# The last 272 token columns of a closing two-matmul stage: second product with the weights stationary, in place of two token tiles and a 16-column strip

## The chip, the cores and the metric

The kernel runs on one NeuronCore of a Trainium2 chip. The metric is the device time of one execution in microseconds; the time before is the median of three runs. One further execution was recorded by the profiler, and all rows below come from it. PE is TensorE (matmuls), PEld its weight loads, DVE is VectorE, ACT is ScalarE, POOL is GpSimd, SP issues DMAs.

## The reference

Three stages follow one another: attention with rotary embedding, a top-1 mixture of eight experts, and a two-matmul stage. Only the last is touched by the change:

```python
def _moe2_ref(x, w_in, w_out, alpha):        # x 1152x512, w_in 512x2048, w_out 2048x512, float64 weights
    h = x @ w_in
    g = np.maximum(h, 0.0) + alpha * np.minimum(h, 0.0)
    return (g @ w_out).astype(np.float32)
```

A token that its expert had no room for has a row of zeros, so only the tokens that were kept need this stage. In the path that runs here they fill at most 784 columns.

## The kernel before

All of the closing stage is in `ffn` (made by `make_ffn`). The tokens stand as columns: `yh` holds the 512 features of up to 784 tokens, split into a high and a low part. Each product runs in three passes (high by high, high by low, low by high), the tuple `PASS`.

**The first product** is `up(f)`, for f from 0 to 15: 128 of the 2048 hidden features at a time, the weights stationary, the tokens moving in three blocks of 272, 256 and 256 columns. One block is 12 matmuls into one of four PSUM banks. ACT reads the bank twice (L1133, L1134: the positive and the negative part into temporary tiles of `room`), DVE joins the two with alpha (L1136), ACT rounds the result to the high part of g (L1141), and POOL forms the low part (L1142). g of one f lies in one of five slots (`g01`, `split_room`).

**The second product** is `down(mg)`, for mg from 0 to 3: four f at a time, with g stationary. A token tile is 128 columns of g; 12 matmuls with 512 columns of w_out moving make its 128 x 512 partial output in one PSUM bank, and DVE scales it and adds it to an accumulator (L1198, L1200). There are six tiles, 0 to 5, and they go round three banks, `acc[0]` to `acc[2]`: tile 3 can start when DVE has read tile 0, tile 4 when it has read tile 1.

**The strip.** 784 is six tiles and 16 columns. The 16 columns (`STRIP`) are kept unsplit in float32: POOL copies them out of the third block (L1146), and `down_strip`, behind tile 0 of each `down`, multiplies them with the unsplit w_out in four column groups of the array (L1157), into the fourth bank, `acc[3]`. Only then may the next w_out block be loaded over the unsplit one (`load2`). In the last `down` ACT copies the bank out (L1166) and a matmul with the 0/1 matrix `fold` adds the four column groups (L1171, behind tile 3). `fold` is made by a DVE reduction in the first microseconds of the program (L993).

**The weights** arrive as float64. A piece, `split2`, makes 128 x 512 of them usable: three DVE instructions turn the bits into float32 (L1020, L1021, L1022), ACT rounds them (L1025), POOL forms the low part (L1026). There are 24 pieces in this path of the stage. `pace()` is called behind each block of `up` and each tile of `down`, and every second call puts one piece into the queues (`piece`); four of the pieces fall within each of the first three `down`s and the last `up` ahead of it, none into the last `down`.

**The order.** Every engine runs its queue in the order in which the code writes it. The stage is up(0) to up(4), down(0), up(5) to up(8), down(1), up(9) to up(12), down(2), up(13) to up(15), down(3). In down(3) each finished tile is scattered to the rows of `out` by an indirect DMA that POOL issues (L598). Below, down(0) to down(3) are called the first to the fourth pass.

## Time and profile before

| what | value |
|---|---|
| median of 3 runs | 464.43 us (464.12 to 465.53) |
| the profiled execution's own time | 468.51 us |
| its span, first to last instruction | 466.7 us |
| mean granted TensorE clock | 0.982 |
| PE busy | 421.9 us, 90% |
| DVE busy | 305.5 us, 65% |
| ACT busy | 216.1 us, 46% |
| POOL busy | 238.7 us, 51% |
| closing stage | from 302.07 us to the end |

A share of busy time is an average over stages with different limits. The closing stage has three kinds of stretches: those of the first product, the first three passes of the second product with weight pieces on DVE beside them, and the fourth pass without. What ends a wait is read in each by itself. A row of the order of time gives the start in us, the duration in us, engine, line, operation, the tiles written and read, the shape, the count, and in brackets the idle time before it with the instruction that ended it.

### The profile page before, as it was taken

The page shows a single profiled execution, that of the slowest core. Times are in us where ns is not written, and L with a number is a line of the kernel's source. Part 1 is how long each engine was busy: PE and PEld are TensorE (multiplying, and loading weights), DVE is VectorE, ACT ScalarE, POOL GpSimd, SP SyncE. Part 2 cuts the span into 40 slices and gives each one's busy share as a digit, 9 for nine tenths or more (in the row PEclk, how much of TensorE's full clock was granted, in tenths as well). Part 3 has the DMA queues.
Part 4 walks back from the last instruction along what each step waited for, and adds up shares of the span by engine and source line. Part 5 has one row for each costly group of instructions (what it writes and reads, how often), then busy time and mean ns, then how long its engine had stood idle before and what let it go on. Part 6 is the DMA issues. An engine that isn't in the chain of part 4 may idle for free. (4 is left out here: it accounts for less than half of the span.)

```text
span 466.7 us, 8223 instructions
## 1 busy us (share of the span) xinstructions
PE 421.9 (90%) x2993; PEld 332.2 (71%) x2993; DVE 305.5 (65%) x563; ACT 216.1 (46%) x540; POOL 238.7 (51%) x280
## 2 busy tenths in 40 slices
PE   6789999999989999995878798998999899889993
PEld 3576666666666666695867798697689589758962
DVE  8996566574777464579489911139888797886321
ACT  2476767666665667342253331164424514432600
POOL 6578482864775334148645310047736745662532
PEclk9999999999999999999899898999999999999998
DMA  7422999604031624467466667940314045000012
GB/s 215 129 60 48 175 332 295 185 1 121 0 119 35 195 88 160 158 228 250 104 208 216 235 222 264 374 170 1 122 60 180 5 178 183 0 1 0 2 69 73
DMA packets 37329, 63.71 MB, mean 137 GB/s; under 512 B 9886, under 2 KB 16158, under 8 KB 37280
## 3 DMA queue, kind: packets, MB, share of 16 engines
q1 hardware_dynamic: 35424, 58.83, 39.7%
q0 software_dynamic: 1568, 3.95, 2.3%
q8 instruction: 25, 0.41, 0.4%
q10 hardware_dynamic: 288, 0.33, 0.2%
q14 instruction: 24, 0.20, 0.1%
HBM read 47.35 MB, written 11.65 MB: 126 GB/s over the span
## 5 line engine op out<-in xcount | busy, mean ns | idle before, releaser
L308 DVE TENSOR_REDUCE nm<-S 128x1 f32<-128x576 f32 x72 | 54.2, 755 | 45.0 <-PE S L299 27.7
L309 ACT ACTIVATE P<-S,nm 128x576 f32<-128x576 f32 x72 | 53.5, 742 | 52.6 <-DVE nm L308 51.0
L1124 PE MATMUL u_a<-yh,whl 128*128 128x256 f32 (+1 forms) x576 | 71.3, 284 | 6.1 <-ACT room L1134 5.7
L1124 PEld LDWEIGHTS u_a<-yh,whl 128*128 128x128 f32 x576 | 70.1, 188 | 7.4 <-ACT room L1134 6.4
L1136 DVE SCALAR_TENSOR_TENSOR room<-room,nal 128x256 f32<-128x256 f32 (+1 forms) x48 | 30.5, 637 | 30.9 <-ACT room L1134 30.8
L330 PEld LDWEIGHTS pt<-ident,P 128*128 128x128 f32 x256 | 27.0, 141 | 29.3 <-ACT P L309 6.8
L1026 POOL TENSOR_TENSOR whl<-wraw,whl 128x512 fp32r<-128x512 f32 x22 | 28.9, 1312 | 35.8 <-ACT whl L1025 32.7
L363 PE MATMUL av<-PT,v 128*64 128x288 f32 x256 | 44.7, 431 | 0.4 <-DVE PT L319 0.3
L1188 PE MATMUL acc<-whl,split_room 128*128 128x512 f32 x162 | 42.3, 396 | 2.2 <-DVE xs L1200 1.2
L330 PE MATMUL pt<-ident,P 128*128 128x128 f32 x256 | 41.5, 286 | 3.1 <-ACT P L309 2.9
L1025 ACT CAST whl<-wraw 128x512 fp32r<-128x512 f32 x22 | 14.5, 657 | 54.2 <-DVE wraw L1022 54.2
L1188 PEld LDWEIGHTS acc<-whl,split_room 128*128 128x128 f32 x162 | 29.7, 188 | 13.1 <-DVE xs L1200 2.9
L1142 POOL TENSOR_TENSOR g<-room,g 128x272 fp32r<-128x272 f32 (+2 forms) x21 | 17.7, 853 | 41.7 <-ACT g L1141 39.2
L299 PE MATMUL S<-T,T 128*128 128x288 f32 x112 | 36.1, 338 | 1.1 <-DVE T L178 1.1
L1188 PE MATMUL acc<-whl,g 128*128 128x512 f32 x126 | 32.9, 391 | 0.5 <-POOL whl L1026 0.5
L299 PE MATMUL S<-X,T 128*128 128x288 f32 x112 | 31.2, 293 | 0.0
L154 POOL TENSOR_TENSOR hl<-R,hl 128x512 fp32r<-128x512 f32 x12 | 15.4, 1287 | 30.6 <-ACT hl L153 30.5
L1142 POOL TENSOR_TENSOR split_room<-room,split_room 128x272 fp32r<-128x272 f32 (+2 forms) x27 | 24.6, 919 | 12.3 <-ACT split_room L1141 9.5
L1188 PEld LDWEIGHTS acc<-whl,g 128*128 128x128 f32 x126 | 23.5, 188 | 6.6 <-POOL whl L1026 0.9
L319 DVE COPY PT<-pt 128x512 f32<-128x512 f32 (+1 forms) x32 | 19.9, 623 | 12.2 <-PE pt L330 7.9
L319 ACT COPY PT<-pt 128x512 f32<-128x512 f32 (+1 forms) x48 | 26.0, 544 | 3.6 <-PE pt L330 3.4
L927 POOL TENSOR_TENSOR whl<-wraw,whl 128x512 fp32r<-128x512 f32 x12 | 15.9, 1329 | 22.3 <-ACT whl L924 22.3
(290 smaller groups left out, 925.4 us busy)
## 6 DMA issues: line engine op xcount, KB each, us to landing
wraw<-moe_w SPq DMA_DIRECT2D x16, 1024.0 KB, 6.3
wraw<-moe_w_out SPq DMA_DIRECT2D x3, 2048.0 KB, 8.1
x_disp<-zero SPq DMA_DIRECT2D x9, 576.0 KB, 8.0
wraw<-moe_w_in SPq DMA_DIRECT2D x2, 2048.0 KB, 10.1
X<-T SPq DMA_DIRECT2D x14, 288.0 KB, 4.1
room<-moe_w SPq DMA_DIRECT2D x3, 1024.0 KB, 6.5
out<-zero SPq DMA_DIRECT2D x4, 576.0 KB, 7.9
v<-v SPq DMA_DIRECT2D x8, 256.0 KB, 5.2
```

Of the source, the lines that this page charges most:

```text
L299: nc.tensor.matmul(ps[:, half, 0:288], lhsT=lhsT, rhs=rhs, start=(n == 0), stop=(n == len(terms) - 1),)
L308: nc.vector.tensor_reduce(nm, ps[:, :, 0:288], op=ALU.max, axis=AX.XY, negate=True)
L309: nc.scalar.activation(Pt.rearrange("p (a n) -> p a n", a=2), ps[:, :, 0:288], AF.Exp, bias=nm, scale=1.0, accum_out=st["ssum"][:, t, hh : ...
L319: (nc.vector.tensor_copy if SCH["e"][k] else nc.scalar.copy)(o, i)
L330: nc.tensor.transpose(ps[:, kb, :], Pt[:, at : at + 128], ident)
L363: nc.tensor.matmul(ps[64 * hh : 64 * hh + 64, 0:288], lhsT=lhs, rhs=(PT[:, hh, kb] if kb < 4 else PR)[:, half * 288 : half * 288 + 288], s ...
L927: eng.tensor_tensor(ht[:, 1, c], rt[:, c], ht[:, 0, c].bitcast(F32), op=ALU.subtract)
L1026: nc.gpsimd.tensor_tensor(ht[:, 1, c], hw.bitcast(F32), ht[:, 0, c].bitcast(F32), op=ALU.subtract)
L1124: nc.tensor.matmul(ps, lhsT=wt[:, a, c, (f % 4) * 128 : (f % 4) * 128 + 128], rhs=yh_[0][:, b, c, c0 + lo : c0 + hi], start=(c == 0 and i ...
L1136: nc.vector.scalar_tensor_tensor(A, Bn, nal[:, f : f + 1], A, op0=ALU.mult, op1=ALU.add)
L1142: nc.gpsimd.tensor_tensor(g_cols(g, 1, lo, mid), A[:, 0 : mid - lo], hi_.bitcast(F32), op=ALU.subtract)
L1188: nc.tensor.matmul(ps[:m], lhsT=g_cols(g, b, t * P, t * P + m), rhs=wt[:, a, c, :], start=(c == 0 and i == 0), stop=(c == 3 and i == 2),)
```

## The change

The three blocks of the first product become 256, 256 and 272 columns. The 16 columns are no longer held apart: the last block of 272 columns (`TURN`) is split into high and low parts like the others, and the g slots are 784 columns wide instead of 768. Tiles 0 to 3 stay as they were. In place of tiles 4, 5 and the strip, `down_turned` runs behind tile 1 of each pass: for each d of four 128-column groups of w_out, 12 matmuls with w_out stationary and the 272 columns of g moving make a 128 x 272 block of the transposed output, and DVE adds it to the accumulator `accT`. All groups go round four banks instead of three. In the fourth pass, ahead of tile 3, `finish_turned` transposes `accT` back on PE, four 128 x 128 transposes for each of tiles 4, 5 and 6 (the last with 16 rows), DVE scales each, and POOL scatters it. `pace()` is called as often as before in each pass. The loads of w_out no longer wait for the strip, the reduction for `fold` is gone, and the memory that was zeroed for the strip by DVE is replaced by a part of `accT` zeroed by POOL.

```diff
+TURN = 256 + STRIP
...
-        nc.vector.tensor_reduce(
-            fold, ident.rearrange("p (g m) -> p m g", m=32)[:, 0:STRIP], op=ALU.add, axis=AX.X
-        )
...
-                            if c == 3 and not (strip and g % 2):
+                            if c == 3:
                                 later.append(lambda: load2(seq.index(g) + 2))
...
-                                if mid < hi:
-                                    nc.gpsimd.tensor_copy(gs[:, f // 4 % 2, f % 4, 0:STRIP], A[:, mid - lo : hi - lo])
...
+                    def down_turned(mg):
+
+                        wt = w2_hl(2 * mg + 1)
+                        for d in range(4):
+                            ps = po(f"t_{tag}_{mg}_{d}")[:, 0:TURN]
+                            for c in range(4):
+                                g = gt[(4 * mg + c) % NG]
+                                for i, (a, b) in enumerate(PASS):
+                                    nc.tensor.matmul(
+                                        ps,
+                                        lhsT=wt[:, a, c, d * 128 : d * 128 + 128],
+                                        rhs=g_cols(g, b, c_t, n_all),
+                                        start=(c == 0 and i == 0),
+                                        stop=(c == 3 and i == 2),
+                                    )
+                            flush()
+                            o = accT[:, d, 0:TURN]
+                            if mg == 0:
+                                nc.vector.tensor_copy(o, ps)
+                            else:
+                                nc.vector.tensor_tensor(o, ps, o, op=ALU.add)
+                            if d % 2:
+                                pace()
+
+                    def finish_turned(t, m):
+
+                        at = t * P - c_t
+                        ps = po(f"y_{tag}_{t}")
+                        for d in range(4):
+                            nc.tensor.transpose(ps[:, d * 128 : d * 128 + 128], accT[:, d, at : at + 128], ident)
+                        y = A_y[t][:m]
+                        nc.vector.tensor_scalar(y, ps[:m], wgt[:m, t, 0:1], None, op0=ALU.mult)
+                        finish(t, m, y)
...
                         for t, m in tiles:
-                            if strip and t == 1:
-                                down_strip(mg)
+                            if turned and t == 2:
+                                down_turned(mg)
+                            if mg == 3 and t == 3:
+                                for last in turned:
+                                    finish_turned(*last)
...
-                                if strip and t == 3:
-                                    finish_strip()
...
-                    ffn(0, (272, 256, 256), "a", False, (0, 1))
+                    ffn(0, (256, 256, TURN), "a", False, (0, 1))
...
-                u, d = itertools.cycle(("h", "xt")), itertools.cycle(range(3))
+                u, d = itertools.cycle(("h", "xt")), itertools.cycle(range(4))
```

The third pass on PE, before: acc_2502, acc_2503 and acc_2504 are the three banks, acc_2505 the strip's, whl the split weights, g and split_room the slots of g.

```order
L1188 MATMUL acc_2502<-whl_2101,split_room 128x512 x6
L1188 MATMUL acc_2502<-whl_2101,g_2104 128x512 x6
L1157 MATMUL acc_2505<-wraw_2100,room 32x512 x4
L1188 MATMUL acc_2503<-whl_2101,split_room 128x512 x6
L1188 MATMUL acc_2503<-whl_2101,g_2104 128x512 x6
L1188 MATMUL acc_2504<-whl_2101,split_room 128x512 x6
L1188 MATMUL acc_2504<-whl_2101,g_2104 128x512 x6
L1188 MATMUL acc_2502<-whl_2101,split_room 128x512 x6
```

The same pass on PE now, from tile 1 to the first half of tile 2; the four banks are acc_2500 to acc_2503, and tile 0, not shown, is in acc_2500.

```order
L1196 MATMUL acc_2501<-whl_2099,split_room 128x512 x6
L1196 MATMUL acc_2501<-whl_2099,g_2102 128x512 x6
L1154 MATMUL acc_2502<-split_room,whl_2099 128x272 x6
L1154 MATMUL acc_2502<-g_2102,whl_2099 128x272 x6
L1154 MATMUL acc_2503<-split_room,whl_2099 128x272 x6
L1154 MATMUL acc_2503<-g_2102,whl_2099 128x272 x6
L1154 MATMUL acc_2500<-split_room,whl_2099 128x272 x6
L1154 MATMUL acc_2500<-g_2102,whl_2099 128x272 x6
L1154 MATMUL acc_2501<-split_room,whl_2099 128x272 x6
L1154 MATMUL acc_2501<-g_2102,whl_2099 128x272 x6
L1196 MATMUL acc_2502<-whl_2099,split_room 128x512 x6
```

Behind tile 0 the strip is gone; tile 1 and two short groups now come ahead of the group that takes tile 0's bank again.

DVE in the third pass, before, from the reading of tile 0 (acc_2502) to that of tile 5; the rows on wraw are weight pieces.

```order
L1200 SCALAR_TENSOR_TENSOR xs<-acc_2502,room,xs 128x512
L1020 TENSOR_SCALAR cv<-wraw_2483 128x512
L1021 SCALAR_TENSOR_TENSOR wraw_2483<-wraw_2483,cv 128x512
L1022 SCALAR_TENSOR_TENSOR wraw_2483<-wraw_2483 128x512
L1200 SCALAR_TENSOR_TENSOR xs<-acc_2503,room,xs 128x512
L1200 SCALAR_TENSOR_TENSOR xs<-acc_2504,room,xs 128x512
L1020 TENSOR_SCALAR cv<-wraw_2483 128x512
L1021 SCALAR_TENSOR_TENSOR wraw_2483<-wraw_2483,cv 128x512
L1022 SCALAR_TENSOR_TENSOR wraw_2483<-wraw_2483 128x512
L1200 SCALAR_TENSOR_TENSOR room<-acc_2502,room 128x512
L1200 SCALAR_TENSOR_TENSOR room<-acc_2503,room 128x512
L1200 SCALAR_TENSOR_TENSOR room<-acc_2504,room 128x512
```

DVE in the same pass now, from the reading of tile 1 (acc_2501) to that of tile 3.

```order
L1208 SCALAR_TENSOR_TENSOR xs<-acc_2501,room,xs 128x512
L1166 TENSOR_TENSOR room<-acc_2502,room 128x272
L1166 TENSOR_TENSOR room<-acc_2503,room 128x272
L1017 TENSOR_SCALAR cv<-wraw_2481 128x512
L1018 SCALAR_TENSOR_TENSOR wraw_2481<-wraw_2481,cv 128x512
L1019 SCALAR_TENSOR_TENSOR wraw_2481<-wraw_2481 128x512
L1166 TENSOR_TENSOR room<-acc_2500,room 128x272
L1166 TENSOR_TENSOR room<-acc_2501,room 128x272
L1208 SCALAR_TENSOR_TENSOR xs<-acc_2502,room,xs 128x512
L1208 SCALAR_TENSOR_TENSOR room<-acc_2503,room 128x512
```

The place of the pieces among the readings stays: one behind the reading of tile 0, one behind the reading of bank 3.

The end of the fourth pass on PE now, from the third short group: tile 2, the transposes of tiles 4, 5 and 6, and tile 3.

```order
L1154 MATMUL acc_2500<-split_room,whl_2100 128x272 x9
L1154 MATMUL acc_2500<-g_2102,whl_2100 128x272 x3
L1154 MATMUL acc_2501<-split_room,whl_2100 128x272 x9
L1154 MATMUL acc_2501<-g_2102,whl_2100 128x272 x3
L1196 MATMUL acc_2502<-whl_2100,split_room 128x512 x9
L1196 MATMUL acc_2502<-whl_2100,g_2102 128x512 x3
L1175 MATMUL acc_2503<-ident,room 128x128 x4
L1175 MATMUL acc_2500<-ident,room 128x128 x4
L1175 MATMUL acc_2501<-ident,room 128x128 x4
L1196 MATMUL acc_2502<-whl_2100,split_room 128x512 x9
L1196 MATMUL acc_2502<-whl_2100,g_2102 128x512 x3
```

Five of the seven scatters, of tiles 2, 4, 5, 6 and 3 in this order, now stand behind the last two tiles; before, each of the seven stood behind a tile of its own or the `fold` matmul.

## Rows read from the trace of the kernel before

**Rows 1.** The page, busy time of each engine over the span (us, share, instructions).

```profile
PE 421.9 (90%) x2993; PEld 332.2 (71%) x2993; DVE 305.5 (65%) x563; ACT 216.1 (46%) x540; POOL 238.7 (51%) x280
```

**Rows 2.** Busy us by stretch (PE, PEld, DVE, ACT, POOL), granted clock, DMA: third, fourth pass.

```profile
405.00:427.00 22.00, 19.50 (x83) 13.57 (x82) 18.42 (x24) 7.21 (x18) 12.20 (x12) 1.00 0.00 1
...
440.00:460.00 20.00, 19.24 (x85) 13.71 (x83) 5.85 (x9) 1.94 (x5) 8.12 (x10) 1.00 0.18 67
```

**Rows 3.** Order of time on PE, second pass: strip, tile 1, next first product.

```profile
369.55 1.10 PE L1157 MATMUL acc<-wraw,room 128*32 128x512 f32 x6
...
372.03 0.98 PE L1188 MATMUL acc<-whl,split_room 128*128 128x512 f32 x3
...
385.80 14.65 PE L1124 MATMUL u_a<-yh,whl 128*128 128x272 f32 x120
```

**Rows 4.** Order of time on PE, third pass: strip, tiles 1 and 4, next first product.

```profile
408.68 1.10 PE L1157 MATMUL acc<-wraw,room 128*32 128x512 f32 x6
...
411.59 1.66 PE L1188 MATMUL acc<-whl,split_room 128*128 128x512 f32 x6
...
421.56 1.65 PE L1188 MATMUL acc<-whl,split_room 128*128 128x512 f32 x6 [0.80 <-DVE xs L1200]
...
427.13 13.16 PE L1124 MATMUL u_a<-yh,whl 128*128 128x272 f32 x108
```

**Rows 5.** Order of time on DVE: readings of tiles 0, 1 and 2, a piece's start.

```profile
374.40 0.74 DVE L1200 SCALAR_TENSOR_TENSOR xs<-acc,room,xs 128x512 f32<-128x512 f32 x1
...
378.22 1.41 DVE L1200 SCALAR_TENSOR_TENSOR xs<-acc,room,xs 128x512 f32<-128x512 f32 x2
...
416.96 0.74 DVE L1200 SCALAR_TENSOR_TENSOR xs<-acc,room,xs 128x512 f32<-128x512 f32 x1
417.62 1.38 DVE L1020 TENSOR_SCALAR cv<-wraw 128x512 uint32<-128x512 uint32 x1
...
420.76 1.40 DVE L1200 SCALAR_TENSOR_TENSOR xs<-acc,room,xs 128x512 f32<-128x512 f32 x2
```

**Rows 6.** Order of time on PE, fourth pass: strip, tiles 2 and 3, fold.

```profile
442.95 1.26 PE L1157 MATMUL acc<-wraw,room 128*32 128x512 f32 x8
...
447.00 2.20 PE L1188 MATMUL acc<-whl,split_room 128*128 128x512 f32 x9
...
449.72 2.20 PE L1188 MATMUL acc<-whl,split_room 128*128 128x512 f32 x9
...
452.53 1.03 PE L1171 MATMUL acc<-wraw,fold 128*16 128x512 f32 x2
```

**Rows 7.** Order of time on PE in the attention: four float32 transposes.

```profile
151.34 0.66 PE L330 MATMUL pt<-ident,P 128*128 128x128 f32 x4
```

**Rows 8.** Order of time: last reading on DVE, its scatter, and scatters in a row.

```profile
229.45 0.97 POOL L598 DMA_INDIRECT meta_d<-g_meta,m_mi  x1 [0.30 <-issue]
...
459.27 0.75 DVE L1200 SCALAR_TENSOR_TENSOR room<-acc,room 128x512 f32<-128x512 f32 x1 [1.97 <-PE acc L1188]
...
460.30 0.97 POOL L598 DMA_INDIRECT out<-room  x1 [1.73 <-POOLq L1604]
```

**Rows 9.** Order of time on DVE at the program's start: the fold reduction.

```profile
3.82 0.26 DVE L993 TENSOR_REDUCE fold<-ident 128x16 f32<-128x64 f32 x1
```

**Rows 10.** Costliest groups on the page (count, busy us, mean ns, idle before): POOL copies, whole stage.

```profile
L1146 POOL COPY room<-room 128x16 f32<-128x16 f32 x16 | 7.4, 462 | 0.0
```

**Rows 11.** PE idle stretches in order of time, and the stretch after each, as Rows 2.

```profile
281.87 0.40 PE L1258 MATMUL xs<-ident,xs 32*128 32x32 f32 x4 [1.84 <-DMA xs<-x_disp]
...
282.00:288.00 6.00, 6.00 (x34) 5.96 (x34) 0.52 (x2) 0.29 (x1) 0.00 (x0) 0.72 0.73 229
325.32 0.86 PE L1124 MATMUL u_a<-yh,whl 128*128 128x256 f32 x5 [2.33 <-ACT room L1134]
...
325.00:327.00 2.00, 1.68 (x13) 1.69 (x14) 1.97 (x2) 0.57 (x2) 2.00 (x2) 1.00 0.00 0
```

More of the change, by code (lines that the diff above doesn't have):

```diff
@@ L870, in build @@
         nc.vector.memset(x_tok[:, 1, 4, 0:256], 0.0)
-        fold = cp.tile([P, STRIP], F32, name="fold")
         al = cp.tile([P, 16], F32, name="al")
@@ L951, in first_work @@
             xs_[0] = ep.tile([P, 3, 512], F32, name="xs")
-            g01 = hl["g"] = ep.tile([P, 4 * (NCOL - STRIP)], F32R, name="g01")
+            g01 = hl["g"] = ep.tile([P, 4 * NCOL], F32R, name="g01")
             xT[0] = g01[:, 0 : 8 * W].rearrange("p (b c n) -> p b c n", b=2, c=4)
@@ L1041, in src2, with make_ffn @@
                 return w_out[mg * 512 : mg * 512 + 512, :]
[L1043 to L1047 removed]
+            def make_ffn(zp, gp, tp, pf, po):
+                acc3, accT = zp("acc3", [P, 512]), zp("accT", [P, 4, 3 * P])
+                acc2 = lambda t, m: xs_[0][:m, t] if t < 3 else acc3[:m]
+                NG, NG_COLS = 5, NCOL
                 gt = [hl["g"][:, i * 2 * NG_COLS : (i + 1) * 2 * NG_COLS] for i in range(2)]
@@ L1059, in ffn @@
                     tiles = [(t, min(P, n_all - t * P)) for t in range(-(-n_all // P))]
-                    strip = tiles.pop() if n_all % P == STRIP else None
-                    if strip:
-                        side = pt(f"side_{tag}")
-                        nc.vector.memset(gs, 0.0)
+                    c_t = edges[-2] if blocks[-1] == TURN else n_all
+                    turned = [(t, m) for t, m in tiles if t * P >= c_t]
+                    if turned:
+                        nc.gpsimd.memset(accT[:, :, TURN:], 0.0)
+                    tiles = [(t, m) for t, m in tiles if t * P < c_t]
                     done, later = [0, 0], []
@@ L1136, in up, with rest @@
                             nc.vector.scalar_tensor_tensor(A, Bn, nal[:, f : f + 1], A, op0=ALU.mult, op1=ALU.add)
-                            def rest(A=A, g=g, lo=lo, hi=hi, f=f):
-                                mid = min(hi, NCOL - STRIP) if strip else hi
-                                hi_ = g_cols(g, 0, lo, mid)
-                                nc.scalar.copy(hi_, A[:, 0 : mid - lo])
-                                nc.gpsimd.tensor_tensor(
-                                    g_cols(g, 1, lo, mid), A[:, 0 : mid - lo], hi_.bitcast(F32), op=ALU.subtract
-                                )
-                                if mid < hi:
-                                    nc.gpsimd.tensor_copy(gs[:, f // 4 % 2, f % 4, 0:STRIP], A[:, mid - lo : hi - lo])
+                            def rest(A=A, g=g, lo=lo, hi=hi):
+                                hi_ = g_cols(g, 0, lo, hi)
+                                nc.scalar.copy(hi_, A)
+                                nc.gpsimd.tensor_tensor(g_cols(g, 1, lo, hi), A, hi_.bitcast(F32), op=ALU.subtract)
                             later.append(rest)
@@ L1152, in finish @@
                         gate.scatter(out, wgt[:m, t, 1:2].bitcast(I32), src, "out" + tag)
-                    def down_strip(mg):
-                        for c in range(4):
-                            nc.tensor.matmul(
-                                side[32 * c : 32 * c + 32],
-                                lhsT=gs[:, mg % 2, c],
-                                rhs=src_of(2 * mg + 1, c)[:, :, 1].bitcast(F32),
-                                start=(mg == 0),
-                                stop=(mg == 3),
-                            )
-                        load2(seq.index(2 * mg + 1) + 2)
-                        if mg == 3:
-                            nc.scalar.copy(strip_out[0], side)
@@ L1168, in finish_strip @@
-                    def finish_strip():
-                        t, m = strip
-                        ps = po("d_strip")
-                        nc.tensor.matmul(ps[:m], lhsT=fold, rhs=strip_out[0], start=True, stop=True)
-                        y = strip_out[0][:m]
+                    def down_turned(mg):
[20 more added lines that the diff above has]
+                                pace()
@@ L1178, in down @@
+                    A_y = {t: spent[:, i * 512 : i * 512 + 512] for i, (t, _) in enumerate(turned)}
                     def down(mg):
@@ L1230, in build @@
                 room = mp.tile([P, 4864], F32, name="room")
-                split_room = mp.tile([P, 4608], F32R, name="split_room")
+                split_room = mp.tile([P, 6 * NCOL], F32R, name="split_room")
                 rawx = room[:, 0:2048].bitcast(U32).rearrange("p (c f w) -> p c f w", c=2, w=2)
```

19 lines of the change are left out of this document (6 added, 13 removed).

## The prediction

> **What bounds the kernel now.** I read the page first: PE is busy for 90% of the span, DVE for 65% [rows 1]. That average hides stages with different limits, so the next view is the busy time by stretch, one for each part of the closing stage. In the third pass DVE is busy for 18.42 of 22 us and PE for 19.50; in the fourth DVE has 5.85 of 20 us and PE 19.24 [rows 2]. So the first three passes have two limits close together, PE and the weight pieces on DVE, and the fourth has PE alone. The order of time on PE and DVE then shows which wait ends last: in the third pass PE stands 0.80 us ahead of tile 4, until DVE has read tile 1 out of the same bank [rows 4]. DVE reads that tile at 420.76, long after its matmuls, because a weight piece that starts at 417.62 is ahead of it in the queue [rows 5]. This is where the reader should look: the strip is PE work, but while PE does it DVE catches up.
>
> **What goes from PE.** Each pass loses its strip. From strip start to tile 1 it takes 372.03 - 369.55 = 2.48 us in the second pass [rows 3] and 411.59 - 408.68 = 2.91 in the third [rows 4], waits for POOL's copies included; the first is taken as the second. In the fourth it is 1.26, and the fold matmuls are 1.03 [rows 6]. That is 2.48 + 2.48 + 2.91 + 1.26 + 1.03 = 10.2 us.
>
> **What comes to PE.** Two tiles of 2.72 us (449.72 - 447.00 [rows 6]) become four groups of 12 matmuls with 272 columns. Blocks of the first product have that form, with the same 128 x 128 weight loads: 120 of them, 262 columns on average, take 14.65 us [rows 3], 122 ns each, so a group of 12 with 272 columns is 1.5 us. Four are 6.0 instead of 5.44, 0.56 more a pass. Weight loads that don't hide are excluded by the same row. Transposes: four take at most 0.66 us with their pipeline's end [rows 7]; in a row I take 0.5, so 1.5 for the twelve. If nothing else stood in the way, PE would gain 10.2 - 4 x 0.56 - 1.5 = 6.5 us.
>
> **Why it doesn't get them: the banks.** Replay the third pass with the durations of the rows. Tile 1 starts where the strip did, 408.68, and ends at 411.40. The first two short groups end at 412.90 and 414.40, in the third and fourth bank. The third short group takes tile 0's bank again, and DVE reads that tile at 416.96 for 0.74 us [rows 5]; nothing in the change moves this reading, since the pieces ahead of it are those of before. So PE stands from 414.40 to 417.76 (with 0.06 us from the reading's end to PE, as at tile 4). The third group ends at 419.26. The fourth takes tile 1's bank, which DVE reads behind the next piece, at 420.76 for 0.75: PE stands until 421.56, as before the change [rows 4, 5]. From here on the old order had two tiles left, 5.44 us; the new has a short group and two tiles, 1.5 + 5.44. It ends at 428.50 instead of 427.13: **+1.37 us**. Four banks run less far ahead than three did, because two of the groups are short and the strip is gone: ahead of the wait for tile 0 there are now 5.44 + 3.0 = 8.4 us of matmuls, and there were three tiles and a strip, 8.16 + 2.9 = 11.1.
>
> The second pass goes the same way. Tile 1 ends at 372.27, the short groups at 373.77, 375.27 and, since tile 0's bank is free at 375.14 [rows 5], 376.77. The fourth waits for tile 1, read at 378.22 for 0.75: PE stands until 379.03, and the pass ends at 379.03 + 1.5 + 5.44 = 385.97 instead of 385.80 [rows 3, 5]: +0.2. The first pass is taken as the second. Whether the blocks behind them pass such a shift on or absorb it is open; PE waits for ACT there once in each (2.33 us at 325.32 [rows 11]), which is ACT behind the pieces. I take +0.2 for both together, between 0 and +0.4.
>
> The readings of the short groups, four of 272 columns a pass, take the place of two of 512. Their price lies between half of 0.75 and 0.75 us; even at 0.75 those of the first two end ahead of the groups that need their banks again, and cost nothing.
>
> **The fourth pass** has no pieces, so the saving shows: -1.26 - 1.03 + 0.56 + 1.5 = **-0.2**. But its end moves onto POOL. A scatter follows a reading by 0.28 us (460.30 - 459.27 - 0.75), and scatters in a row start 0.97 + 0.30 = 1.27 us apart [rows 8]. Let tile 2's matmuls end at T. Its scatter starts at T + 1.07; those of 4, 5, 6 and 3 follow, and the last starts at T + 1.07 + 5.08 = T + 6.15. Tile 3's matmuls end at T + 1.5 + 2.72, and its scatter would be ready at T + 5.3. POOL's queue adds **+0.85**. Behind the last scatter the program's end is the same.
>
> **Small things.** The fold reduction, 0.26 us of DVE at the start [rows 9], is on a busy engine: 0 to -0.26, taken -0.2. POOL's 16 copies, 7.4 us [rows 10], go, 16 columns move into the low-part operations; POOL is off the path, and what DVE gains is a rival below. The earlier loads of w_out change nothing in the sum: between 417.62 and 420.76 DVE shows no wait for data [rows 5]. The zeroing that POOL gets lies ahead of its first operation of the stage. ACT loses one copy that nobody but the fold waited for.
>
> **The clock.** The granted clock fell to the lower of its two levels (1.2 and 2.4 GHz) after an idle stretch of 1.84 us at 281.87: 282 to 288 has a mean of 0.72, so 6 x 0.28 x 2 = 3.4 us at half rate. It didn't after 2.33 us at 325.32 [rows 11]. The changed third pass has idle stretches of 3.4 and 2.3 us with 1.5 us of matmuls between, more than any in this stage now, so I expect a fall. 3.4 us at half rate cost 1.7 us of work; where 2.3 of them fall into the second wait, (3.4 - 2.3) / 2 = 0.55. I take **+0.6**, between 0 and 1.7 for each fall. The Trainium skill (TensorE: Matmul & The Clock Gate, section "Why this matters for your kernels") advises against idle gaps of PE between bursts of matmuls for this reason; by that rule the fall is sure, by the rows it is likely.
>
> **The sum.** +1.37 + 0.2 - 0.2 + 0.85 - 0.2 + 0.6 = +2.6 us. On the profiled execution, 468.5 becomes 471.1, nearly all of it in the span; the median of the runs shown is 4.1 us lower, and I take the same difference there: 464.43 + 2.6 = **467.0**. The ends of its own terms give 465.9 (no fall) to 468.3.
>
> **Rivals.**
> - *The gain shows.* If DVE's readings of tiles 0 and 1 come early enough, passes 1 to 3 gain 2.48 + 2.48 + 2.91 - 3 x 0.56 = 6.2 us, and the sum is -6.2 - 0.2 + 0.85 - 0.2 = -5.8: 458.6. It begins to be faster once tile 1 is read some 2 us earlier in each pass. For it: POOL's copies, 462 ns each, run beside the pieces, and without them DVE could be faster. Against it: they are 7.4 us over the whole stage, under 2 a pass, not all beside DVE. The Trainium skill (Perfetto Trace Analysis, section "Matmuls") says that groups should rotate through different PSUM banks so that the reading of one overlaps the matmuls of the next; by this rule a fourth bank should shorten the waits. Rows 4 and 5 say that the reading engine is behind, not the number of banks. From 458.6 to 463.0, chance 0.13.
> - *No change to speak of.* The blocks of the first product give the shift back (PE waits for ACT there anyway), or DVE gains 1 us a pass from the missing copies: +1.37 shrinks to about 0, and what is left is POOL's queue and the clock. 463.1 to 465.8, chance 0.17.
> - *The clock falls again and again.* The first two passes have idle stretches of 2.2 us too. Two to four falls that cost 1.7 each instead of the 0.6 give +2.0 + 3.4 to +2.0 + 6.8: 468.4 to 473. Chance 0.20.
>
> **How the numbers follow.** The forecast, slower by waits for banks and POOL's queue, has 0.50. About 0.3% is what a measurement of this kernel can tell from no change: 463.0 to 465.8. So faster 0.13, same 0.17, slower 0.50 + 0.20 = 0.70. The range leaves out the first rival and the upper half of the clock's: 463.0 to 470.5.
>
> **What would show it.** On PE in the third pass, idle stretches ahead of the third and fourth short group of 3.4 and 2.3 us, ended by DVE's readings; in the first two passes one of 2.2 us ahead of the fourth. The first product after the third pass starts about 1.4 us later than 427.13. No strip, twelve transposes in 1.5 us. The last five scatters 1.27 us apart, the last one's wait ended by POOL itself. The forecast is wrong if the third and fourth short groups start without a wait, or if tile 1's reading comes well before 420 in the third pass.

## The result, and the profile after

The changed kernel takes 467.62 us in the median, the kernel before 464.35: a ratio of **1.0059**, 95% interval 1.0036 to 1.0083, so by the ratio it is 2.7 us slower. Here and below the medians take in all executions and the ratios leave out those in a slower state of the chip (two of the changed kernel's 20, whose median is 467.25 us without them, one of the six of e2 and three of the twelve of e6). The prediction was 467.0, slower by 2.6 us. The total is right; whether its terms are is another question, and two of them are not.

The four groups of 12 matmuls with 272 columns in a pass are called short groups below; a record is the trace of one execution. The four passes come first, each from its first matmul to the next first product's (the fourth to PE's last matmul): stretch, length, busy time of PE, PEld, DVE, ACT and POOL, granted clock, share and rate of DMA. Before:

```profile
326.84:346.65 19.81, 18.94 (x82) 13.73 (x81) 17.14 (x23) 6.55 (x17) 11.13 (x12) 1.00 0.30 107
365.97:385.80 19.83, 18.98 (x82) 13.72 (x81) 16.98 (x24) 6.58 (x17) 10.63 (x11) 1.00 0.28 106
405.10:427.13 22.03, 19.53 (x82) 13.57 (x81) 18.32 (x24) 7.21 (x18) 12.20 (x12) 1.00 0.00 1
440.13:459.23 19.10, 19.10 (x84) 13.58 (x82) 5.00 (x8) 1.94 (x5) 8.07 (x10) 1.00 0.16 60
```

And after:

```profile
322.13:341.32 19.19, 18.51 (x98) 15.93 (x97) 16.64 (x24) 6.49 (x18) 10.21 (x10) 0.94 0.31 111
360.64:380.75 20.11, 17.78 (x99) 15.08 (x97) 16.83 (x26) 6.64 (x17) 9.37 (x9) 1.00 0.28 106
400.11:425.24 25.13, 20.42 (x98) 17.33 (x97) 18.15 (x26) 7.29 (x18) 11.00 (x10) 0.86 0.00 1
438.30:456.95 18.65, 18.65 (x110) 16.14 (x108) 6.48 (x11) 1.40 (x4) 6.50 (x8) 1.00 0.14 50
```

PE has 1.2 us less work in the second pass (18.98 to 17.78), yet the pass is 0.28 us longer: the strip's time has become waiting. The third pass is 3.10 us longer, at a granted clock of 0.86; the fourth, which has no pieces, is 0.45 shorter. The first product between the passes is as long as before (19.32 and 19.36 us, before 19.32 and 19.30). The stretch ahead of this stage moves by some us from one record to the next (the stage begins at 302.07 before, at 296.76 after), in runs that share its code too, so passes are compared by their own lengths.

PE's order of time in the third pass after (start, length, line, operation; in brackets the idle time ahead and what ended it), from the second short group to the next first product; [rows 4] are its counterpart:

```profile
408.48 0.91 PE L1154 MATMUL acc<-g,whl 128*128 128x272 f32 x6
412.59 1.21 PE L1154 MATMUL acc<-split_room,whl 128*128 128x272 f32 x6 [3.19 <-DVE xs L1208]
413.60 1.56 PE L1154 MATMUL acc<-g,whl 128*128 128x272 f32 x6
416.44 1.73 PE L1154 MATMUL acc<-split_room,whl 128*128 128x272 f32 x6 [1.28 <-DVE xs L1208]
417.96 1.56 PE L1154 MATMUL acc<-g,whl 128*128 128x272 f32 x6
419.32 1.90 PE L1196 MATMUL acc<-whl,split_room 128*128 128x512 f32 x6
...
425.24 1.00 PE L1121 MATMUL u_a<-yh,whl 128*128 128x256 f32 x7
```

DVE over the same time, as [rows 5]: a piece's first operation, the readings of tile 0 and tile 1 (L1208) with a piece between them, and the first two short groups' readings (L1166):

```profile
408.77 0.42 DVE L1017 TENSOR_SCALAR cv<-wraw 128x512 uint32<-128x512 uint32 x1
...
411.79 0.74 DVE L1208 SCALAR_TENSOR_TENSOR xs<-acc,room,xs 128x512 f32<-128x512 f32 x1
412.45 1.35 DVE L1017 TENSOR_SCALAR cv<-wraw 128x512 uint32<-128x512 uint32 x1
413.91 1.08 DVE L1018 SCALAR_TENSOR_TENSOR wraw<-wraw,cv 128x512 uint32<-128x512 uint32 x1
415.02 0.69 DVE L1019 SCALAR_TENSOR_TENSOR wraw<-wraw 128x512 uint32<-128x512 uint32 x1
415.63 0.74 DVE L1208 SCALAR_TENSOR_TENSOR xs<-acc,room,xs 128x512 f32<-128x512 f32 x1
416.30 0.78 DVE L1166 TENSOR_TENSOR room<-acc,room 128x272 f32<-128x272 f32 x2
```

The third short group starts 0.06 us after tile 0's reading ends (411.79 + 0.74), the fourth 0.07 after tile 1's. Counted from the pass's start, the readings lie where they lay: 11.68 and 15.52 us, before 11.86 and 15.66 [rows 4, 5]. Six matmuls of a short group take 0.75 us until 409.3, and 1.36 at 417.96. The clock says why (stretches of this pass, columns as above):

```profile
413.00:416.00 3.00, 2.16 (x11) 1.84 (x10) 2.86 (x4) 0.25 (x1) 1.44 (x2) 0.54 0.00 0
416.00:420.00 4.00, 3.56 (x14) 3.47 (x15) 3.86 (x8) 0.78 (x2) 1.30 (x1) 0.50 0.01 2
420.00:424.00 4.00, 4.00 (x18) 3.23 (x18) 1.04 (x2) 0.30 (x1) 1.31 (x1) 0.99 0.00 0
```

After the wait of 3.19 us PE is granted the lower of its two levels (1.2 of 2.4 GHz) until about 420, and most of that time it is at work. At the end of the program, the last reading on DVE and the last two scatters on POOL, as [rows 8]:

```profile
456.99 0.75 DVE L1208 SCALAR_TENSOR_TENSOR room<-acc,room 128x512 f32<-128x512 f32 x1 [1.41 <-PE acc L1196]
457.72 0.88 POOL L599 DMA_INDIRECT out<-wraw,room  x1 [0.30 <-issue]
458.91 0.98 POOL L599 DMA_INDIRECT out<-room  x1 [0.30 <-issue]
```

The last scatter starts 1.17 us after its reading ends, not 0.28, and what it waits for is POOL itself: it starts 0.30 us after the end of the scatter ahead of it.

The first pass has a fall of the clock too (0.94 above), behind a wait for ACT ahead of the pass; the wait for a bank ahead of the fourth short group is then 0.68 us:

```profile
320.05 2.29 PE L1121 MATMUL u_a<-yh,whl 128*128 128x272 f32 x12 [2.46 <-ACT room L1131]
...
334.14 1.03 PE L1154 MATMUL acc<-g,whl 128*128 128x272 f32 x6 [0.68 <-DVE xs L1206]
```

So every wait that the prediction named is there, with its length off in one: 0.68 us in the first pass, where 2.2 was expected.

### The profile page after: what moved, and what is told of

Same layout as the page of the kernel before. It is cut to its first block, busy times and chain, and to the rows that moved or that the text cites. A ratio compares the mean times of both kernels' runs of the same rounds, so it can differ in the third digit from the quotient of the medians.

```text
span 464.6 us, 8357 instructions
## 1 busy us (share of the span) xinstructions
PE 420.0 (90%) x3067; PEld 342.3 (74%) x3067; DVE 306.3 (66%) x571; ACT 216.0 (47%) x539; POOL 233.5 (50%) x265
## 4 chain that ended last, share of the span: by engine, by line
PE 55%; DVE 24%; issue 8%; POOL 4%; DMA 4%; ACT 3%; DVEq 1%; another core or an unknown queue 0%; POOLq 0%; ACTq 0%
PE av L364 10%; PE u_a L1121 9%; PE S L300 9%; PE pt L331 7%; DVE cv L1017 4%; PE acc L1196 4%; DVE room L1133 3%; DVE wraw L1018 3%; PE xl L387 3%; PE pT L191 2%; DMA xs<-x_disp 2%; DVE wraw L1019 2%; DVE rawy L1018 2%; POOL yh L1500 1%; PE acc L1470 1%
## 5 line engine op out<-in xcount | busy, mean ns | idle before, releaser
L1138 POOL TENSOR_TENSOR split_room<-room,split_room 128x256 fp32r<-128x256 f32 (+1 forms) x27 | 24.6, 913 | 17.1 <-ACT split_room L1137 12.9
L1196 PE MATMUL acc<-whl,split_room 128*128 128x512 f32 x108 | 28.7, 400 | 0.2 <-POOL whl L1023 0.2
L1130 ACT ACTIVATE room<-u_a 128x256 f32<-128x256 f32 (+1 forms) x48 | 18.6, 388 | 20.1 <-PE u_a L1121 20.1
L1138 POOL TENSOR_TENSOR g<-room,g 128x256 fp32r<-128x256 f32 (+1 forms) x21 | 18.0, 863 | 12.0 <-ACT g L1137 9.1
L1196 PEld LDWEIGHTS acc<-whl,split_room 128*128 128x128 f32 x108 | 20.3, 193 | 4.8 <-POOL whl L1023 0.7
L1196 PE MATMUL acc<-whl,g 128*128 128x512 f32 x84 | 23.5, 411 | 0.2 <-POOL whl L1023 0.2
```

The source lines that it names most:

```text
L1138: nc.gpsimd.tensor_tensor(g_cols(g, 1, lo, hi), A, hi_.bitcast(F32), op=ALU.subtract)
L1196: nc.tensor.matmul(ps[:m], lhsT=g_cols(g, b, t * P, t * P + m), rhs=wt[:, a, c, :], start=(c == 0 and i == 0), stop=(c == 3 and i == 2),)
```

## The experiments

The theory: (1) PE waits for banks that DVE reads late, because pieces stand ahead of the readings; (2) the clock falls behind these waits; (3) POOL's queue delays the end. Rivals: the short groups are dear in themselves, PE alone is the limit, or the banks only show a limit that is DVE's.

**e4: the kernel before, strip left out.** What was the strip worth?

```diff
-                        for c in range(4):
-                            nc.tensor.matmul(
-                                side[32 * c : 32 * c + 32],
-                                lhsT=gs[:, mg % 2, c],
-                                rhs=src_of(2 * mg + 1, c)[:, :, 1].bitcast(F32),
-                                start=(mg == 0),
-                                stop=(mg == 3),
-                            )
                         load2(seq.index(2 * mg + 1) + 2)
-                        if mg == 3:
-                            nc.scalar.copy(strip_out[0], side)
...
-                                if strip and t == 3:
-                                    finish_strip()
```

> The kernel before without its strip: the strip matmuls of the four passes, the copy of their bank, the fold matmul and the last 16 columns' result are left out, so those 16 tokens have no result; POOL's copies and the loads stay where they are. Bank theory: in the third pass PE stands about 3.6 us ahead of tile 3 and 1.1 ahead of tile 4 instead, and ends at the same time; the second pass gains 1.3 us, the first about as much, the fourth 2.3: -4.9 us, ratio 0.989, up to 1.8 us less gain where the clock falls behind the new wait (0.993). Rival, PE alone is the limit and the strip costs what its time on PE is: -10.2 us, ratio 0.978.

Measured: 461.61 us, ratio 0.9948 (0.9913 to 0.9982), -2.4 us of the strip's 10.2 by the ratio, less than the 3.1 to 4.9 that the bank theory expected. PE alone isn't the limit. Two waits of its trace, in the third pass and in the first product before it:

```profile
396.35 4.63 PE L1124 MATMUL u_a<-yh,whl 128*128 128x256 f32 x24 [1.97 <-ACT room L1134]
...
411.93 1.65 PE L1178 MATMUL acc<-whl,split_room 128*128 128x512 f32 x6 [2.77 <-DVE xs L1190]
```

The passes are 1.1, 1.2, 1.6 and 2.6 us shorter (18.67, 18.59, 20.47 and 16.49), but the first products between them 1.2 and 2.7 longer (20.55, 22.02, the latter with a fall of the clock). Of the 6.5 us that the passes gain, the next first products give back 4.0. The passes themselves come out as expected but for the third, which gains 1.6 us where nothing was expected (its wait is 2.77 us, not 3.6); what I lacked is what the first products do.

**e1: two more banks for the short groups.**

```diff
-                            ps = po(f"t_{tag}_{mg}_{d}")[:, 0:TURN]
+                            ps = (pf if d > 1 and mg < 3 else po)(f"t_{tag}_{mg}_{d}")[:, 0:TURN]
```

> The changed kernel, but in the first three passes the third and fourth short group go into two banks of the first product, which are free by then; nothing else differs. Bank theory: PE's waits ahead of these two groups go (0.68 us in the first pass, 2.08 in the second, 3.19 + 1.28 in the third), what comes back is at most about 1.4 us ahead of tiles 2 and 3 of the third pass, whose banks wait for the readings of tiles 0 and 1. 4 to 6 us less than the changed kernel, so a ratio to the kernel before of 0.993 to 0.997. Rival, the pieces on DVE are the limit and the banks only show it: PE gets to the next first product early and stands there instead; within 0.5 us of the changed kernel, 1.004 to 1.008. Rival, the turned groups themselves are dear: nothing changes, 1.006.

Measured: 458.3 us, ratio **0.9886** (0.9849 to 0.9922), faster than both kernels and better than expected. Third pass, and the first product ahead of it:

```profile
391.34 3.21 PE L1121 MATMUL u_a<-yh,whl 128*128 128x272 f32 x24 [1.72 <-ACT room L1131]
396.43 3.20 PE L1121 MATMUL u_a<-yh,whl 128*128 128x256 f32 x24 [1.89 <-ACT room L1131]
...
411.97 1.67 PE L1196 MATMUL acc<-whl,split_room 128*128 128x512 f32 x6 [0.26 <-DVE xs L1208]
...
415.82 1.67 PE L1196 MATMUL acc<-whl,split_room 128*128 128x512 f32 x6 [0.80 <-DVE xs L1208]
```

The short groups wait no more; the first three passes take 17.26, 17.67 and 19.28 us, at a clock of 0.99 to 1.00. Together that is 10.2 us less than in the changed kernel's record (1.93 + 2.44 + 5.85, some 1.6 of the last being the fall of the clock, see e5 and e11). The first products between them take 20.14 and 21.55, 0.8 and 2.2 us longer. So the rival that DVE is behind is true in part: it takes back 3.0 us.

**e7: the kernel before, with these two banks** for tiles 2 and 3 of the first three passes.

```diff
-                            ps = po(f"d_{tag}_{mg}_{t}")
+                            ps = (pf if t in (2, 3) and mg < 3 else po)(f"d_{tag}_{mg}_{t}")
```

> The kernel before, strip and all, with tiles 2 and 3 of the first three passes in two banks of the first product, as the short groups of the run named e1. Theory: there the waits for banks are small (0.80 us in the third pass), since the strip is matmul time that lies in them; so banks alone bring at most 1 us, ratio 0.998 to 1.000, and the 0.9886 of that run needs both, the strip gone and the banks. Rival, more banks bring the gain in either form: 0.988 to 0.992.

Measured: 462.69 us, 0.9971 (0.9933 to 1.0010). The third pass is 20.21 instead of 22.03, more than the 0.80 expected; the first two are as before. The kernel before has a second wait for a bank in that pass, ahead of tile 3, which the prediction and this expectation passed over:

```profile
417.76 1.65 PE L1188 MATMUL acc<-whl,split_room 128*128 128x512 f32 x6 [0.43 <-DVE xs L1200]
```

In the kernel before two banks bring 0.3%, which the interval can't tell from nothing; in the changed kernel, without the strip and with short groups, they bring 1.7% (e1 against it).

**e9: three banks for the changed kernel**, `itertools.cycle(range(3))` for `range(4)`.

> The changed kernel with its tiles and short groups in three banks, as the kernel before had, instead of four. Bank theory: each group needs a bank whose reading stands behind a piece one group earlier, about 1.5 us more in each of the first three passes (second short group behind tile 0, third behind tile 1) and about 0.5 at the transposes, of which the first products give back up to 2: 2.5 to 5 us more than the changed kernel, ratio to the kernel before 1.011 to 1.017. Rival, DVE alone sets the pace and the number of banks doesn't matter: 1.006 as the changed kernel.

Measured: 472.82 us, 1.0190 (1.0146 to 1.0234). The first and second pass take 21.14 and 21.61 us (with four banks 19.7 and 20.1, in e2 and e11 below), 1.5 more each, as expected; the third takes 27.39, with a longer fall of the clock in it, and the total is above the range expected. Three, four and six banks: 1.019, 1.006, 0.989.

**e10: the piece behind tile 1's reading**, four banks.

```diff
+                        pace()
...
-                            pace()
+                            if not (turned and t == 0):
+                                pace()
```

(The first is at the end of `down_turned`, the second behind a tile's reading in `down`.)

> The changed kernel, its four banks, but the weight piece that stands between the readings of tiles 0 and 1 comes behind the reading of tile 1 (one slot later, as the pieces behind it); as many pieces in each pass. Theory, the wait of the fourth short group is this piece: it goes (0.7, 2.1 and 1.3 to 2.1 us), tile 2 waits about 1 us for the first short group's reading instead in the second and third pass; 2 to 3 us less than the changed kernel, ratio to the kernel before 0.999 to 1.002. The wait of the third short group in the third pass (3.2 us) stays, since tile 0's reading is as late as before. Rival, what DVE does later only moves the wait: 1.006.

Measured: 464.03 us, 0.9983 (0.9948 to 1.0018), as expected. No bank is added; only a piece is moved by one slot, and the loss is gone. The first three passes take 17.85, 17.14 and 22.69 us, and again the first products between them take some of it back (21.97, with a fall of the clock, and 20.21). The third pass, third and fourth short group and tile 2:

```profile
412.80 1.55 PE L1154 MATMUL acc<-split_room,whl 128*128 128x272 f32 x6 [3.23 <-DVE xs L1209]
414.15 1.56 PE L1154 MATMUL acc<-g,whl 128*128 128x272 f32 x6
415.51 1.34 PE L1154 MATMUL acc<-split_room,whl 128*128 128x272 f32 x6
416.69 0.92 PE L1154 MATMUL acc<-g,whl 128*128 128x272 f32 x6
417.45 1.55 PE L1197 MATMUL acc<-whl,split_room 128*128 128x512 f32 x6
```

The wait for tile 1 is gone, that for tile 0 stays, with a fall of the clock behind it (6 matmuls take 1.35 us), and the stall that was expected ahead of tile 2 in the second and third pass didn't come. This shows the cause of the fourth group's wait: the piece between the two readings.

**e5 and e11: matmuls in the waits.** Behind the second and third short group PE multiplies into a bank that nobody reads; e5 does it in the third pass (24 and 16 matmuls), e11 in all three, with this edit:

```diff
+                            extra = {(0, 2): 5, (1, 2): 16, (2, 1): 24, (2, 2): 16}.get((mg, d), 0)
+                            if extra:
+                                busy = pf(f"busy_{tag}_{mg}_{d}")[:, 0:TURN]
+                                for i in range(extra):
+                                    nc.tensor.matmul(
+                                        busy, lhsT=wt[:, 0, 0, 0:128], rhs=g_cols(gt[4 * mg % NG], 0, c_t, n_all),
+                                        start=True, stop=True,
+                                    )
```

> The changed kernel with 24 + 16 extra matmuls (3.0 and 2.0 us, into a bank of the first product that nobody reads) in the third pass, behind the second and the third short group, where PE otherwise stands for 3.2 us and about 2.5. They change no result. Clock theory: they cost nothing while PE would wait, the granted clock stays at 1.00 in that pass, which takes 23.4 us and not 25.1; 0.6 to 1.75 us less than the changed kernel, ratio to the kernel before 1.002 to 1.0045. Rival, the fall costs nothing since it lies in the waits: 1.006, or above where the extra matmuls push the groups back.

> The changed kernel with extra matmuls that change no result in the waits of all three passes (5, 16 and 24 + 16, which is 0.6, 2.0 and 3.0 + 2.0 us). Records so far show a fall of the clock behind the third pass's wait in 3 of 3 (25.1 us with, 23.5 without) and behind the second's in 2 of 4 (21.6 with, 20.1 without). Clock theory: the granted clock stays at 1.00 in the passes, 1.5 us for each fall, two falls of the usual two or three gone: 2 to 3 us less than the changed kernel, ratio 0.999 to 1.002. Rival, the falls come elsewhere instead or are too few to show in the time: 1.004 to 1.006.

Measured: e5 466.29 us, 1.0071 (1.0037 to 1.0105), a miss; e11 465.58 us, 1.0020 (0.9983 to 1.0056), at the edge of what was expected, with the rival's 1.004 inside the interval too. The intervals overlap each other and that of the changed kernel, so the times alone don't settle it. The traces do for the third pass; here e11's extra matmuls, and the first half of the third and of the fourth short group behind them:

```profile
410.88 3.19 PE L1173 MATMUL busy_a<-split_room,whl 128*128 128x272 f32 x24
414.30 1.03 PE L1154 MATMUL acc<-split_room,whl 128*128 128x272 f32 x6 [0.22 <-DVE xs L1216]
...
415.91 2.19 PE L1173 MATMUL busy_a<-split_room,whl 128*128 128x272 f32 x16
418.17 1.01 PE L1154 MATMUL acc<-split_room,whl 128*128 128x272 f32 x6
```

And that pass as a stretch, columns as above:

```profile
401.77:425.33 23.56, 23.03 (x138) 20.14 (x137) 18.25 (x26) 7.31 (x18) 11.08 (x10) 1.00 0.00 1
```

With the extra work the pass takes 23.56 us (23.55 in e5) at a clock of 1.00; without it 25.13, 25.13 and 25.03 in the three records of this form (the changed kernel, e2, e6), with a fall in each. The fall costs 1.5 to 1.6 us. The second pass, whose wait of 2.08 us e5 doesn't fill, takes 20.1 us in the records of the changed kernel and e2, and 21.6 and 21.7 in those of e5 and e6, where the clock falls behind that wait. That is how e5's own record loses again what its third pass gains; why e5's twelve times show no gain, one record can't say.

**e2: the short groups of the fourth pass ahead of tile 0, e3: the edits of e1 and e2 together.**

```diff
-                            if turned and t == 2:
+                            if turned and t == (0 if mg == 3 else 2):
                                 down_turned(mg)
-                            if mg == 3 and t == 3:
+                            if mg == 3 and t == 1:
```

> The changed kernel, but in the fourth pass the short groups stand ahead of tile 0 and the twelve transposes ahead of tile 1; passes 1 to 3 are untouched. Scatter theory: POOL has sent the three scatters of the short groups before tiles 2 and 3 are read, the last scatter follows its reading by about 0.28 us and not by 1.17, 0.85 us less than the changed kernel: ratio to the kernel before 1.004. Rival, POOL's queue isn't what ends last (program end hangs on something else): 1.006 as the changed kernel.

> Both edits, of the two runs named e1 and e2. If the two terms are apart, their sum: 5 to 7 us less than the changed kernel, ratio to the kernel before 0.991 to 0.995. If the pieces on DVE are the limit: 1.002 to 1.006.

Both miss. e2: 470.08 us, 1.0130 (1.0074 to 1.0186); e3: 461.84, 0.9965 (0.9930 to 1.0000), worse than e1. The last scatter does follow its reading by 0.28 us, but the fourth pass takes 20.49 us and not 18.65. The wait is new: the last 272 columns are those that the first product has just made, and the first short group stands for them:

```profile
441.76 0.39 PE L1154 MATMUL acc<-g,whl 128*128 128x272 f32 x1 [0.69 <-ACT g L1137]
...
442.68 0.52 PE L1154 MATMUL acc<-g,whl 128*128 128x272 f32 x2 [0.53 <-POOL g L1138]
```

**e6: three scatters left out**, the call of `finish` at the end of `finish_turned`.

> The changed kernel without the three scatters of the short groups, so 272 tokens have no result; the transposes and readings stay. POOL's queue theory as in the prediction: the last scatter follows its reading at once, 0.85 us less: ratio to the kernel before 1.004, and from PE's last matmul to the program's end 6.7 us and not 7.55. Rival, from the first four runs: those 0.85 us lie within the program's end anyway, which took 7.4 to 7.9 us from PE's last matmul whether the last scatter was queued or not: 1.006, and 7.4 to 7.6 us.

Measured: 468.34 us, 1.0058 (1.0021 to 1.0095): no gain, as the rival said. The last two scatters on POOL in its trace, whose span is 466.8 us:

```profile
456.35 0.97 POOL L599 DMA_INDIRECT out<-xs,room  x1 [7.83 <-DVE xs L1207]
460.47 0.97 POOL L599 DMA_INDIRECT out<-room  x1 [3.15 <-POOLq L1606]
```

And PE's last row there:

```profile
458.55 0.86 PE L1195 MATMUL acc<-whl,g 128*128 128x512 f32 x3
```

The last scatter waits for no other here, and from PE's end (458.55 + 0.86) the program still takes 7.4 us; in the changed kernel 464.6 - 456.95 = 7.6, in the kernel before 466.7 - 459.23 = 7.5. Over the fourteen records it is 7.7 in the mean where the last scatter was queued (eight) and 7.6 where it was not (six).

**e8: e1 with a third of the pieces' DVE operations left out** (L1018 of each piece).

> The kernel of the run named e1 with the second of the three DVE operations of every weight piece left out, so the weights are not the right numbers. Theory: behind each pass PE now stands 1.6 to 2.4 us ahead of a block of the first product, because DVE is behind with pieces; with 0.7 to 1.0 us less for each piece these waits shrink and 2 to 4 us go: ratio 0.980 to 0.985. Rival, those waits hang on ACT's own chain, not on the pieces: 0.9886 as that run.

Measured: 442.79 us, 0.9552 (0.9501 to 0.9603), 15.5 us less than e1. The direction is the theory's, the size isn't. A first product and the pass behind it:

```profile
332.85:350.24 17.39, 17.39 (x145) 17.39 (x144) 12.71 (x17) 9.11 (x26) 11.25 (x11) 1.00 0.33 122
350.24:367.38 17.14, 17.14 (x98) 15.08 (x97) 12.89 (x21) 7.40 (x18) 9.42 (x9) 1.00 0.35 124
```

PE is busy without a gap in both; that stretch of the first product took 19.3 us before the change and after it. So DVE is behind in the whole stage, not in the passes alone. The third pass takes 17.20 us, and the waits of 0.26 and 0.80 us that e1 had there for the readings of tiles 0 and 1 are gone: it is the pieces that make these readings late. From its start to PE's last matmul the closing stage takes 140.4 us, in e1's record 153.8: 13.4 of the 15.5 us. (Every piece of the program is lighter, so the stages ahead may gain too; the records can't tell, since the closing stage starts anywhere from 293 to 302 us in them.)

**e12: e1, with ACT reading the banks of the first pass**, `nc.scalar.copy` and `nc.scalar.activation(..., AF.Copy, scale=sc)` for the DVE operations where mg is 0.

> The kernel of the run named e1, but in the first pass, which adds nothing to an older sum, ACT and not DVE reads the four tiles and the four short groups: 4.7 us off DVE, about as much onto ACT, which is busy for 6.6 of 19 us in that pass. If DVE's backlog is the limit in the closing stage, as the run without a third of the pieces' work says: 1 to 3 us less than that run, ratio 0.982 to 0.987. Rival, ACT's queue then holds up the first product's blocks that wait for ACT: 0.9886 or above.

Measured: 459.31 us, 0.9898 (0.9847 to 0.9949): not better than e1, a miss. In the trace the first product after that pass is back at 19.30 us (20.14 in e1), but the next one still takes 21.56: DVE is behind again one pass later. In the time 0.8 us can't be told.

## Why the prediction was right, and where it was not

**PE's work that goes and comes** was right: 12 matmuls of a short group take 1.51 us at the higher level, the twelve transposes 1.22 where 1.5 was taken, and the fourth pass gains 0.45 where 0.2 was expected.

**The banks** were right, and this is what made the change slower rather than faster. Idle stretches of 3.4 and 2.3 us were predicted for the third pass; they are 3.19, and 2.08 in the two records where the clock stayed up until the fourth group. At full clock the pass takes 23.55 us (e5, e11), 1.52 more than before, against +1.37. (The prediction counts one wait for a bank in that pass before, 0.80 us; there are two, 0.43 and 0.80, see e7. Its sum starts from the pass's measured end and isn't touched by that.) For the first two passes +0.2 was taken; in e11, with no fall in this stage, they end 83.95 us after its start, before 83.73. Where no fall lies ahead, the wait before the fourth group is 2.15 in the first pass (e2) and 2.08 in the second, against 2.2. e10 shows the cause of the fourth group's wait, e8 that tile 0's reading too is late because of the pieces, and e9 and e1 that the number of banks sets the price.

**The clock** was too small. The step that failed is the 0.6: I let 2.3 of the 3.4 us at half rate fall into the second wait. In e2 and e6 the fall begins at 419.2 and 420.4, behind the second wait, and none of it lies in a wait. In the changed kernel it begins at about 413.2, ahead of the second wait, which it shortens from 2.08 to 1.28 us, but it lasts twice as long, until 420.0. The third pass loses 1.5 to 1.6 us each time. And the second pass, where no fall was in the sum, has one in two of four records, and the first pass one behind its bank wait in e6. A wait for a bank can hide a fall, but here it does so in the first pass alone: the changed kernel and e5 have a fall ahead of that pass's wait, and from the stage's start to the pass's end they take 44.56 us, as e2 and e11 do without a fall (44.58 and 44.57); in e6, where the fall comes behind the wait, it is 46.13. The rival "the clock falls again and again", with a chance of 0.20, is in part what happened. The Trainium skill's advice against idle gaps between bursts of matmuls (TensorE: Matmul & The Clock Gate, section "Why this matters for your kernels") is borne out by the third pass: the clock falls in all four records with its wait of 3.2 us (the changed kernel, e2, e6, e10).

**POOL's queue** was wrong. The step that failed reads "Behind the last scatter the program's end is the same". The queue is there, 1.17 us instead of 0.28, but from the last scatter's start the program took 5.7 us after (464.6 - 458.91) and 6.4 before (466.7 - 460.30), so +0.85 becomes about +0.1. e6 and e2 agree: without that queue the end comes 7.4 us behind PE's last matmul, 0.2 sooner than in the changed kernel. What the end waits for instead, no row shows; that stays open.

**The fold** (-0.2) can't be seen: the stage's start moves by more than that from record to record.

**The sum again**, from the records: +0.2 (first two passes), +1.5 (banks in the third), -0.45 (fourth pass), +0.1 (end) and +0.1 (first products) make +1.4 us without falls; e11's stage, which has none, takes 158.6 us to PE's last matmul, the kernel before 157.2. (The changed kernel's own record, in which only the third pass's fall costs time, has 160.2, 3.0 more.) With 1.5 us for the fall in the third pass and half as much for one in the second it would be 3.7, and 2.7 was measured; the kernel before may have falls in some of its runs too (none in its record's closing stage, but the granted clock of the runs beside e11 goes from 0.969 to 0.982), and how many isn't known. So 2.6 was right because 0.75 us too much for POOL stood against too little for the clock: the direction and the banks' term were understood, the closeness of the total was luck.

**Slips in the prediction's own sums.** Its terms give about 466.2 to 468.5, not 465.9 to 468.3, and two falls of 1.7 us give 469.8 in the clock's rival, which it lets begin at 468.4. Neither moves the forecast.

**The rival "the gain shows"** fell in this kernel: without POOL's copies tile 0 and 1 are read 0.2 and 0.1 us earlier, not 2. But what I held against the rule on banks was half wrong. The Trainium skill (Perfetto Trace Analysis, section "Matmuls") has groups rotate through banks so that a reading overlaps the next matmuls; I answered that the reading engine is behind, not the number of banks. Both are true: with six banks the reading engine is as far behind (in the third pass PE gets tile 0's bank 12.5 us after the pass's start in e1 as in the changed kernel), and the kernel takes 8 us less (0.9886 against 1.0059).

**The rival "no change to speak of"** fell too: in the changed kernel the first products give nothing back (19.32 and 19.36 us, as before), and in the third pass the readings come 0.2 and 0.1 us earlier, not 1.

**What the first product does with a shift** was left open there. Where the passes get shorter, it takes a part back: 3.0 of 10.2 us in e1, 4.0 of 6.5 in e4 (one fall of the clock among them). e8 says that this part is DVE being behind with the pieces.

## What to carry to other kernels

Work of an engine that is busy for 90% may still stand in another engine's shadow: before it is taken out, replay the stretch with the readings where they are, and see what waits next. When groups get shorter, count the run-ahead in microseconds of matmuls up to the first bank that is needed again, not in banks; here 8.4 us up to tile 0's bank were too few, and with 11.1 the wait for it was 0.43 (e7). And look for the engine that sets the pace of both neighbouring stages: one operation off each weight piece (e8) showed more time to win than all edits to PE.

## What the runs showed of the hardware

Waits of 2.1 us, shorter than the one of 2.33 us that passed without a fall [rows 11], brought a fall of PE's clock in the second pass of two of four records, and the wait of 2.44 to 2.46 us ahead of the first pass was followed by one in the changed kernel, e1 and e5 but not in e2 and e11: the length of a single idle stretch didn't decide it. In the first pass a fall cost nothing where the wait for a bank came behind it, and 1.6 us where it came behind that wait (44.56 and 46.13 us from the stage's start). Matmuls that compute nothing kept the granted clock at 1.00 in the third pass and cost no time in it; in the time of the whole execution that gain can't be told.

DVE's operations on 128x512 uint32 mostly took longer while POOL was at work. Between 200 and 435 us of the changed kernel's record L1017 took 0.41 or 0.42 us all six times that POOL was idle, and 0.83 to 1.50 in 20 of the 26 times that POOL was at work during it, with 0.41 or 0.42 in the other six. Above, it took 0.42 us at 408.77 and 1.35 at 412.45, where POOL's operations of that time are

```profile
412.22 1.31 POOL L1023 TENSOR_TENSOR whl<-wraw,whl 128x512 fp32r<-128x512 f32 x1 [1.31 <-ACT whl L1022]
413.48 0.96 POOL L1138 TENSOR_TENSOR split_room<-room,split_room 128x272 fp32r<-128x272 f32 x1
```

So DVE's backlog may partly be POOL's doing, by its low-part operations rather than by the copies that the change removed. No run here took those away, so whether and how much is open.

The program's end took in a last scatter that starts 0.9 us later: 7.7 us from PE's last matmul in the mean of the records with it, 7.6 without.
